# A recurrent attention kernel: three small transfers issued by another engine, and a reordered first step and tail

## The chip, the cores and the metric

The kernel runs on one core of a Trainium2 chip. Its engines each take their instructions in the order written: TensorE (PE: matmuls and transposes; PEld is the loading of its stationary operand), VectorE (DVE), ScalarE (ACT), GpSimd (POOL) and SyncE (SP). DMA transfers are issued by SP, ACT or POOL as instructions in their own streams (SPq, ACTq, POOLq in the views), and carried by 16 DMA engines. The metric is the time of one execution on the device, in microseconds (us).

## The reference

Two blocks read the same normalized rows, and their results are added to the input:

```
x = A_x                                  # 2048 rows of 1024, bf16
xn = layernorm(x)
out = x + A(xn, mem0, Wq, Wk, Wv, Wo) + B(xn, w_r, w_gate, w_up, w_down)
```

A is attention over 64 segments of 32 rows, one after the other, with a memory of 8 rows that each segment rewrites:

```
for s in range(64):
    h = concat(mem, xn[32 rows of segment s])          # 8 + 32 rows
    q, k, v = h @ Wq, h @ Wk, h @ Wv                   # 32 heads of 128
    o = softmax(mask(q k^T / sqrt(128))) v
    o = o @ Wo
    mem = o[:8];  emit o[8:]
```

B picks the two rows with the largest `xn @ w_r`, sends them through a gated feed-forward block of width 3584, scales each by the sigmoid of its score and adds it to that row; all other rows pass through.

## The kernel before

**Segments and left rows.** A step of the loop handles one segment. The segment's outputs that feed the next memory need only 8 memory rows and its first 24 rows, so each step carries 32 rows: 24 of the segment (XM) and 8 of memory. The last 8 rows of every segment (XL), the "left rows", don't depend on the memory for q, k and v. Their q, k and v are computed once, in the first step, for all 64 segments together (512 rows), and stored in DRAM (`ql_d`, `vl_d`). Every later step loads its piece: QKL (128 KB) and VL (64 KB). In each step the left rows also attend; their sums before the output projection (OTL, 64 KB) are stored to `ol_d`, and all 512 rows are projected through Wo in the tail.

**Phases and granules.** The weights are cut into 64 granules of 128 x 2048 (512 KB). A step has six phases of eight granules: phase p is q, k or v for one half of the heads, in the order of `PHASES`: q half 0, k half 0, q half 1, k half 1, v half 0, v half 1. In a phase 32 matmuls (L745) add to PSm. Granules 48 to 63 are Wo, worked through one by one (`w` 0 to 15, L798). 44 granules stay in SBUF; 17 (`streamed`, among them granules 11 and 15) are fetched anew in each step by SP (L388) from copies in DRAM (`wsc`), into five slots; three are kept in part in PSUM and brought back by copies (BK<-KEPT, L411). In the first step the three kept ones are streamed as well (`first_streamed`). `fetch` puts the next streamed granule into a slot; it has to wait until PE is through with what was there.

**Order by hand.** `manual_schedule` leaves each engine's instructions in the order in which the program writes them. Inside a step, `hook(p, kc, fn)` places work behind granule `kc` of phase `p`: the next rows' load at (2, 0), the store of the last step's sums and the load of VL at (2, 2), the transposes of q or k at granule 3 of the phase after theirs, the scores of half 0 at (2, 6) and of half 1 at (4, 6), the attention products at (5, 3), (5, 6) and within Wo at w 5 and w 8. QKL for the next step is loaded at w 9. A phase's result is cast by ACT (XB, L754), transposed by PE (L632), and copied to QT by ACT (L637) or to KT by ACT (its left columns, L640) and DVE (L642).

**The first step.** Its phases are followed by the left rows' products with the same granules: `left_qk` (L500: 16 heads of eight 512-wide matmuls a phase; results cast by ACT at L502 into GA, in the areas `big0` and `big1`), and `left_v`. After phase 1, in the middle of its left products, come the square roots of 15 row tiles' variances (`sd_rows`), `spread` (four small matmuls that lay means and deviations out by segment, and the copies behind them), and 16 router tiles: for each, DVE normalizes 128 rows into XR (L263) and multiplies and sums them with w_r (L265). After phase 1's left products DVE copies the first segment's QKL out of GA (L513). `left_done(p)` does what follows phase p: fetches for the slots that came free, the loading of the areas, the routing of the two rows. `v_homes` lists the resident v granules; its first eight live in the area `big0`, the ninth is granule 43 (`v_homes[8]`), the last one's room (`hx`) holds the router's temporaries first.

**The tail.** After the last step `left_sums` loads the 512 left rows again (XLS, issued by ACT at L850) and normalizes them on DVE (L238 to L864). `left_rows_out(k)`, called for k = 0 and 1, projects two blocks of 128 left rows each: 64 matmuls a block (L874), whose stationary operand is taken out of OTA, where the 128 rows of one head lie 32 elements apart; then two additions on DVE (L880) and a store. Between the two calls, and behind the second, come the gate and up products of the two routed rows (L903), and at the end the down products (L930). Their weights (MW) are loaded by SP into rooms that come free.

Of the kernel before, what the change touches and what calls it, by code (L numbers as in the profile page):

```python
# [20 lines left out]
NEXT_KEPT = 7  # L21
HALF_KEPT = 27
KEPT_HERE = (FIRST_KEPT, NEXT_KEPT, HALF_KEPT)
NEG = -30000.0

PHASES = [(0, 0), (1, 0), (0, 1), (1, 1), (2, 0), (2, 1)]
# [3 lines left out]
def kernel(  # L30
# [94 lines left out]
    def home(g, shape, dtype, name):  # L125
        return wres.tile(shape, dtype, name=name, tag=f"wres{g}")
# [131 lines left out]

    hx = v_homes[-1]

    def router_tile(t):
        XR = home(hx, [P, D], BF16, "XR")
        nc.vector.tensor_scalar(out=XR[:, :], in0=xt(t), scalar1=RI16[:, t, 0:1], scalar2=RI16[:, t, 1:2],  # L263
                                op0=ALU.subtract, op1=ALU.mult)
        nc.vector.tensor_tensor_reduce(out=XR[:, :], in0=XR[:, :], in1=WRB, scale=1.0, scalar=0.0,  # L265
                                       op0=ALU.mult, op1=ALU.add, accum_out=RF[:, t:t + 1])

    def router_out():
        nc.vector.tensor_copy(out=RB, in_=RF)
# [149 lines left out]
        nc.gpsimd.dma_start(out=granule_out(wsc[g], g), in_=granule_dram(g))  # L419

    to_copy = list(streamed)
    flow += [(s, g) for s in range(NSEG) for g in (streamed if s else first_streamed)]

    moe = [("gu", w, kc, fh) for w in range(2) for kc in range(KC) for fh in range(2)]
    moe += [("dn", fg) for fg in range(FC // 2)]
# [50 lines left out]
    first_half(1)  # L476
    nc.sync.dma_start(out=WRB, in_=B_w_r.unsqueeze(0).to_broadcast([P, D]))
    for g in range(KC, 32):
        if g in first_streamed:
            if len(queued) < N_SLOT:  # L480
                fetch()
        else:
            load_resident(g)
        if g >= 8 and g < 15:
            load_x(g - 7)
    for g in v_homes[8:-1]:
        load_resident(g)
    load_parts()

# [3 lines left out]
    def left_qk(mat, half, Gs, between, h0=0, h1=16):  # L493
        if mat == 0 and h0 == 0:
            gathered[half] = area(f"big{half}", [P, NSEG, 256], "GA")
        GA = gathered[half].rearrange("p s (m i q r) -> p s m i q r", m=2, i=4, q=4)
        for h in range(h0, h1):
            PSG = psA.tile([P, 512], F32, tag="acc", name="PSG")
            for kc in range(KC):
                nc.tensor.matmul(PSG[:, :], lhsT=part(Gs[kc], h // 4)[:, P * (h % 4):P * (h % 4 + 1)], rhs=XLT[:, :, kc, :],  # L500
                                 start=(kc == 0), stop=(kc == KC - 1))
            nc.scalar.copy(out=GA[:, :, mat, h % 4, h // 4, :], in_=PSG.rearrange("p (s r) -> p s r", r=XL))  # L502
            if h % 2 == 1 or mat + half == 0:
                next(between, None)
        if h1 < 16:
            return
        for _ in between:
            pass
        if mat == 1:
            G3 = gathered[half]  # L510
            if half == 0:
                qkl[0] = one.tile([P, 2, 2, 4, 4, XL], BF16, tag="bA", name="QKL")
            nc.vector.tensor_copy(out=qkl[0][:, half].rearrange("p m i q r -> p (m i q r)"), in_=G3[:, 0, :])  # L513
            if half == 0:
                for k in range(NSEG // 8):
                    store_left(half, k)
# [30 lines left out]

    def left_done(p):
        for g in range(8 * p, 8 * (p + 1)):
            if g in first_streamed:  # L550
                fetch()
        if p == 1:
            area("big0", [P, 8, 2048], "W8A")
            for g in AREAS["big0"]:
                load_resident(g)
        elif p == 2:
            router_top()
            route_rows()
        elif p == 3:
            route_turns(*routed[0])  # L560
            load_resident(hx)
            home_first()
        elif p == 4:
            area("big1", [P, 8, 2048], "W8B")
        elif p == 5:
            for g in AREAS["pair"][1:] + [hm]:
                load_resident(g)
        if p in (1, 2):
            copy_blocks(6)
# [14 lines left out]

    def load_qkl(s):
        t = qkl[0] = one.tile([P, 2, 2, 4, 4, XL], BF16, tag="bA", name="QKL")
        nc.gpsimd.dma_start(out=t.rearrange("p h m i q r -> p h (m i q r)"),  # L587
                            in_=ql_d[s // 8][:, :, s % 8].rearrange("h p c -> p h c"))

    def load_vl(s):  # L590
        group["vl"] = one.tile([P, 2, P], BF16, tag="vl", name="VL")
        nc.gpsimd.dma_start(out=group["vl"][:, :, :], in_=vl_d[s // 16][:, s % 16, :, :, :])

    def load_left_out(k, queue):
        queue.dma_start(out=areas["big0"][:, 4 * k:4 * k + 4, :], in_=ol_d[k // 4][4 * (k % 4):4 * (k % 4) + 4].rearrange("s p c -> p s c"))
# [5 lines left out]

    def store_sums():
        s, t = unsaved.pop(0)
        nc.gpsimd.dma_start(out=ol_d[s // 16][s % 16], in_=t.rearrange("p r h -> p (r h)"))


    left_stats()
# [13 lines left out]
    for s in range(NSEG):  # L621
# [7 lines left out]
        def transposes(mat, half, XB):  # L629
            PTq = PTB.rearrange("p (i j r) -> p i j r", i=4, j=4)  # L630
            for il in range(4):
                nc.tensor.transpose(out=PTq[:, il, :, :].rearrange("p j r -> p (j r)"), in_=XB[:, il * P:(il + 1) * P],  # L632
                                    identity=IDENT[:, :])
            pv = PTq.rearrange("p i j r -> p (i j) r")
            if mat == 0:
                QT[half] = one.tile([P, 16, 32], BF16, tag="bE", name="QT")
                nc.scalar.copy(out=QT[half][:, :, :], in_=pv)  # L637
            else:
                KT[half] = one.tile([P, 16, NK], BF16, tag="kt", name="KT")
                nc.scalar.copy(out=KT[half].rearrange("p (i q) k -> p i q k", i=4)[:, :, :, 32:NK],  # L640
                               in_=qkl[0][:, half, 1, :, :, :])
                nc.vector.tensor_copy(out=KT[half][:, :, 0:32], in_=pv)  # L642

        def scores(half):
            QKL = qkl[0]
# [92 lines left out]
        for p, (mat, half) in enumerate(PHASES):  # L738
# [13 lines left out]
            if mat < 2:  # L752
                XB = one.tile([P, 512], BF16, tag=("bE", "kt")[mat], name="XB")
                nc.scalar.copy(out=XB[:, :], in_=PSm[:, :])  # L754
                hooks.setdefault((p + 1, 3), []).insert(0, lambda m=mat, h=half, b=XB: transposes(m, h, b))

                if s == 0:
                    Gs = [Gv_ for _, Gv_ in behind]
                    kept = (x for g_, Gv_ in behind if g_ in KEPT_COLS for x in keep(g_, Gv_))
                    h0, h1 = ((8, 16), (0, 1), (0, 4), (0, 8))[p]  # L760
                    left_qk(mat, half, Gs, kept, h0, h1)
                    if p == 1:
                        nc.gpsimd.tensor_copy(out=GATE, in_=gathered[0][:, 0, 128:132])
                        copy_blocks(6)
                        sd_rows(MV[:, 1:NT, :], VE[:, 1:NT])
                        left_qk(mat, half, Gs, kept, 1, 3)
                        h1 = 3
                        spread(1, NT)
                        for t in range(NT):
                            router_tile(t)  # L770
                    elif p == 2:
                        router_out()
                    elif p == 3:
                        routed.append(route())
                    if h1 < 16:
                        left_qk(mat, half, Gs, kept, h1, 16)
            else:
                VM[half] = one.tile([P, 512], BF16, tag="bA", name="VM")
                nc.scalar.copy(out=VM[half][:, :], in_=PSm[:, :])  # L779

                if s == 0:
                    left_v(half, [Gv_ for _, Gv_ in behind])
# [69 lines left out]
    def left_sums():  # L852
# [7 lines left out]
        for t in range(4):  # L860
# [2 lines left out]
            nc.vector.tensor_scalar(out=r, in0=r, scalar1=1.0, scalar2=None, op0=ALU.add)  # L863
            nc.vector.tensor_scalar(out=left_x(t), in0=left_x(t), scalar1=r, scalar2=m, op0=ALU.mult, op1=ALU.add)  # L864

    OTR = OTA.rearrange("p s (r h) -> p (s r) h", h=H)

    def left_rows_out(k):
        WD = [[psK.tile([P, 512], F32, name=f"WD{2 * b + c}", tag=f"kept{2 * b + c}") for c in range(2)] for b in range(2)]
        for b in range(2):  # L870
            for i, (g, Gv) in enumerate(WOS.items()):
                for hs in range(2):
                    for c in range(2):
                        nc.tensor.matmul(WD[b][c][:, :], lhsT=OTR[:, P * (2 * k + b):P * (2 * k + b + 1), 2 * (g - 48) + hs],  # L874
                                         rhs=Gv[:, D * hs + 512 * c:D * hs + 512 * (c + 1)],
                                         start=(i + hs == 0), stop=(i == 15 and hs == 1))
            x = left_x(2 * k + b)
            for c in range(2):
                xc = x[:, 512 * c:512 * (c + 1)]
                nc.vector.tensor_tensor(out=xc, in0=xc, in1=WD[b][c][:, :], op=ALU.add)  # L880
            nc.scalar.dma_start(out=out2.rearrange("(t s r) d -> t s r d", t=4, s=16)[2 * k + b, :, XM:SEG, :], in_=x)

    T0 = room(resident[2], "T0")
    left_sums()
    left_rows_out(0)
    ROW = T0[:, 0:256]
# [85 lines left out]
```

## Time and profile before

| | us |
|---|---|
| median of 3 runs | 1849.24 (1846.27 to 1857.47) |
| the profiled execution | 1847.92 |
| its span, first to last instruction | 1846.3 |
| first step ends (first L828) | 241.0 |
| last of the 64 steps ends (last L828) | 1759.9 |
| PE busy, of the span | 1555.7 (84%) |
| DVE, ACT, POOL busy | 880.4, 774.9, 320.9 |
| mean granted clock of TensorE | 0.982 |

The rows of the profile are read like this. A line number is a line of the kernel, `out<-in` names its tiles, `xN` counts instructions. In a view in order of time the first column is the start in us from the span's start, the second the duration; a bracket at the end says how long the engine stood idle before it and for whom. In the waits the columns are the sum in us, the count and the longest. In a row of one line the three numbers are the shortest, median and longest duration in ns, then the first and last start. In a row of DMA issues the last two columns are the size of each and the median us from issue to landing.

### The profile page before, as it was taken

The numbers are of one execution on the slowest core, as the hardware profiler recorded it, in microseconds if no ns is written. First come the engines' busy times: TensorE is split into PE (matmuls) and PEld (weight loads), VectorE is DVE, ScalarE is ACT, GpSimd is POOL, SyncE is SP. The second block draws the span as 40 slices with busy tenths as digits, with TensorE's granted clock in tenths as the row PEclk, the third lists the DMA queues.
The fourth block names the chain that finished last, engine by engine and source line by source line (L and its number), as shares of the span: only waits on it lengthen the run. The fifth ranks groups of instructions, "written<-read, shape, count | busy, mean of one in ns | idle before, by whom it ended". The sixth has DMA issues, their size and how long they took to land. (4 is left out here: it accounts for less than half of the span.)

```text
span 1846.3 us, 70379 instructions
## 1 busy us (share of the span) xinstructions
PE 1555.7 (84%) x30358; PEld 828.2 (45%) x30370; DVE 880.4 (48%) x2711; ACT 774.9 (42%) x2019; POOL 320.9 (17%) x592
## 2 busy tenths in 40 slices
PE   6889978888888888888888888888888888888888
PEld 3334434444444444444444444444444444444465
DVE  6631235555554454555555555444455555555420
ACT  2333134444444444444444444444444444444400
POOL 1020111111111111111111111111111111111200
PEclk9999989999999999999999999999999999999988
DMA  9684899999999999999999999999999999999996
GB/s 361 218 301 135 261 367 391 393 394 394 368 387 376 368 389 383 392 386 372 396 393 396 396 394 394 385 386 389 386 391 394 397 382 393 395 395 395 392 364 251
DMA packets 223288, 678.50 MB, mean 367 GB/s; under 512 B 46848, under 2 KB 54320, under 8 KB 222976
## 3 DMA queue, kind: packets, MB, share of 16 engines
q1 hardware_dynamic: 196768, 623.79, 88.3%
q0 software_dynamic: 24192, 46.54, 7.5%
q8 instruction: 237, 3.88, 0.8%
q10 hardware_dynamic: 2016, 3.67, 0.6%
q14 instruction: 75, 0.61, 0.1%
HBM read 652.90 MB, written 29.89 MB: 370 GB/s over the span
## 5 line engine op out<-in xcount | busy, mean ns | idle before, releaser
L745 PE MATMUL PSm<-wres,ST 128*32 128x512 bf16 x6400 | 500.7, 382 | 0.0
L745 PEld LDWEIGHTS <-ST 128*32 128x32 bf16 x12288 | 313.3, 96 | 349.5 <-issue 107.4
L745 PE MATMUL PSm<-g,ST 128*32 128x512 bf16 x3084 | 307.3, 384 | 46.6 <-DMA g<-wsc 38.2
L411 ACT COPY BK<-KEPT 128x512 bf16<-128x512 bf16 x315 | 189.3, 601 | 175.0 <-PE WO L798 65.1
L798 PEld LDWEIGHTS <-OT 128*32 128x32 bf16 x8192 | 209.2, 97 | 85.6 <-issue 69.3
L754 ACT CAST XB<-PSm 128x512 bf16<-128x512 f32 x256 | 150.2, 587 | 132.7 <-PE PSm L745 131.1
L642 DVE COPY KT<-BT 128x512 bf16<-128x512 bf16 x128 | 51.8, 405 | 290.6 <-PE BT L632 290.6
L798 PE MATMUL WO<-W8B,OT 128*32 128x256 bf16 x4096 | 186.2, 276 | 0.0
L745 PE MATMUL PSm<-W8A,ST 128*32 128x512 bf16 x2048 | 182.7, 380 | 0.0
L587 POOL DMA_DIRECT2D QKL<-ql_d x63 | 46.5, 738 | 755.7 <-ACT OTL L714 740.6
L798 PE MATMUL WO<-g,OT 128*32 128x256 bf16 x2560 | 130.7, 277 | 53.1 <-DMA g<-wsc 48.8
L832 POOL DMA_DIRECT2D out_dram<-XN x256 | 130.7, 526 | 173.9 <-DVE XN L828 173.8
L779 ACT CAST VM<-PSm 128x512 bf16<-128x512 f32 x128 | 80.3, 627 | 114.0 <-PE PSm L745 114.0
L411 DVE COPY BK<-KEPT 128x512 bf16<-128x512 bf16 x189 | 80.2, 425 | 72.3 <-ACT BK L411 36.9
L632 PEld LDWEIGHTS <-XB 128*128 128x128 bf16 x1024 | 57.9, 98 | 106.6 <-ACT XB L754 101.5
L674 DVE TENSOR_REDUCE DN<-BS 128x8 f32<-128x320 f32 x128 | 62.9, 491 | 88.0 <-ACT BS L669 88.0
L632 PE MATMUL BT<-IDENT,XB 128*128 128x128 bf16 x1024 | 101.7, 222 | 3.1
L500 PE MATMUL PSG<-XLT,wres 128*128 128x512 bf16 x352 | 101.3, 390 | 0.8 <-ACT GA L502 0.7
L637 ACT COPY QT<-BT 128x512 bf16<-128x512 bf16 x128 | 74.9, 585 | 53.4 <-PE BT L632 51.4
L659 DVE TENSOR_TENSOR BS<-BS,CT 128x96 f32<-128x96 f32 (+1 forms) x256 | 59.7, 233 | 76.5 <-PE BS L652 72.0
L745 PE MATMUL PSm<-BK,ST 128*32 128x512 bf16 x567 | 76.7, 388 | 22.2 <-DVE ST L369 22.2
L828 DVE CAST XN<-WO 128x256 bf16<-128x256 f32 x64 | 27.2, 424 | 127.5 <-PE WO L798 127.5
(171 smaller groups left out, 2278.9 us busy)
## 6 DMA issues: line engine op xcount, KB each, us to landing
g<-wsc SPq DMA_DIRECT2D x1071, 512.0 KB, 6.3
ql_d<-GA POOLq DMA_DIRECT2D x16, 512.0 KB, 6.3
QKL<-ql_d POOLq DMA_DIRECT2D x63, 128.0 KB, 6.2
MW<-in_B_w_gate_dram SPq DMA_DIRECT2D x16, 448.0 KB, 8.0
MW<-in_B_w_down_dram SPq DMA_DIRECT2D x14, 512.0 KB, 8.3
wres<-in_A_Wk_dram SPq DMA_DIRECT2D x12, 512.0 KB, 10.5
MW<-in_B_w_up_dram SPq DMA_DIRECT2D x12, 448.0 KB, 8.5
XP<-in_A_x_dram SPq DMA_DIRECT2D x8, 512.0 KB, 10.1
```

The lines of the kernel that those rows point to most:

```text
L411: copy(out=back[g][c], in_=KEPT_COLS[g][c])
L500: nc.tensor.matmul(PSG[:, :], lhsT=part(Gs[kc], h // 4)[:, P * (h % 4):P * (h % 4 + 1)], rhs=XLT[:, :, kc, :], start=(kc == 0), stop=(kc = ...
L632: nc.tensor.transpose(out=PTq[:, il, :, :].rearrange("p j r -> p (j r)"), in_=XB[:, il * P:(il + 1) * P], identity=IDENT[:, :])
L637: nc.scalar.copy(out=QT[half][:, :, :], in_=pv)
L642: nc.vector.tensor_copy(out=KT[half][:, :, 0:32], in_=pv)
L659: nc.vector.tensor_tensor(out=S4, in0=S4, in1=m, op=ALU.add)
L674: nc.vector.tensor_reduce(out=DN[:, :], in_=S8, axis=AX.X, op=ALU.add)
L745: nc.tensor.matmul(PSm[32 * jq:32 * jq + 32, :], lhsT=ST[:, kc, :], rhs=part(Gv, jq), start=(kc == 0), stop=(kc == KC - 1), tile_position= ...
L754: nc.scalar.copy(out=XB[:, :], in_=PSm[:, :])
L779: nc.scalar.copy(out=VM[half][:, :], in_=PSm[:, :])
L798: nc.tensor.matmul(PS[32 * g:32 * g + 32, 0:256], lhsT=lhs(h), rhs=Gv[:, D * hs + 256 * g:D * hs + 256 * (g + 1)], start=False, stop=(last ...
L832: nc.gpsimd.dma_start(out=out2[s * SEG:s * SEG + XM, 256 * g:256 * (g + 1)], in_=OB[32 * g:32 * g + XM, :])
```

## The change

- In the first step granule 15 (GUEST) is not streamed but loaded with the resident ones, into the room of granule 43; granule 43 is loaded into that room after phase 1.
- `sd_rows` and `spread` for tiles 1 to 15 and the router's tiles move from the middle of phase 1's left products to the end of phase 0's; the tiles alternate between two halves of XR.
- In the first step QKL's copy and the main part of KT's copy are done by ACT, not DVE.
- In all steps QKL's load, VL's load and the store of the left sums are issued by ACT, not POOL.
- In the tail DVE first copies the two heads of a Wo granule for 128 left rows into OCS (eight pieces in turn, in the room that T0 had), and the matmuls of L874 read their stationary operand there, contiguous. T0 moves to another tile.

```diff
-    def router_tile(t):
-        XR = home(hx, [P, D], BF16, "XR")
+    def router_tiles():
+        XR = home(hx, [P, 2, D], BF16, "XR")
+        for t in range(NT):
...
-    flow += [(s, g) for s in range(NSEG) for g in (streamed if s else first_streamed)]
+    flow += [(s, g) for s in range(NSEG) for g in (streamed if s else first_streamed) if s or g != GUEST]
...
     for g in range(KC, 32):
-        if g in first_streamed:
+        if g == GUEST:
+            t = res_tiles[g] = room(v_homes[8], "guest")
+            nc.sync.dma_start(out=t, in_=granule_dram(g))
+        elif g in first_streamed:
             if len(queued) < N_SLOT:
                 fetch()
...
-    for g in v_homes[8:-1]:
+    for g in v_homes[9:-1]:
         load_resident(g)
...
-            nc.vector.tensor_copy(out=qkl[0][:, half].rearrange("p m i q r -> p (m i q r)"), in_=G3[:, 0, :])
+            nc.scalar.copy(out=qkl[0][:, half].rearrange("p m i q r -> p (m i q r)"), in_=G3[:, 0, :])
...
     def left_done(p):
         for g in range(8 * p, 8 * (p + 1)):
-            if g in first_streamed:
+            if g in first_streamed and g != GUEST:
                 fetch()
-        if p == 1:
+        if p == 0:
+            sd_rows(MV[:, 1:NT, :], VE[:, 1:NT])
+            spread(1, NT)
+            router_tiles()
+        elif p == 1:
+            res_tiles.pop(GUEST)
+            load_resident(v_homes[8])
             area("big0", [P, 8, 2048], "W8A")
...
     def load_qkl(s):
-        nc.gpsimd.dma_start(out=t.rearrange("p h m i q r -> p h (m i q r)"),
+        nc.scalar.dma_start(out=t.rearrange("p h m i q r -> p h (m i q r)"),
...
     def load_vl(s):
-        nc.gpsimd.dma_start(out=group["vl"][:, :, :], in_=vl_d[s // 16][:, s % 16, :, :, :])
+        nc.scalar.dma_start(out=group["vl"][:, :, :], in_=vl_d[s // 16][:, s % 16, :, :, :])
...
     def store_sums():
-        nc.gpsimd.dma_start(out=ol_d[s // 16][s % 16], in_=t.rearrange("p r h -> p (r h)"))
+        nc.scalar.dma_start(out=ol_d[s // 16][s % 16], in_=t.rearrange("p r h -> p (r h)"))
...
-                nc.vector.tensor_copy(out=KT[half][:, :, 0:32], in_=pv)
+                (nc.vector.tensor_copy if s else nc.scalar.copy)(out=KT[half][:, :, 0:32], in_=pv)
...
-                        sd_rows(MV[:, 1:NT, :], VE[:, 1:NT])
-                        left_qk(mat, half, Gs, kept, 1, 3)
-                        h1 = 3
-                        spread(1, NT)
-                        for t in range(NT):
-                            router_tile(t)
...
+    OCS = room(resident[2], "OCS").rearrange("p (n h r) -> p n h r", n=8, h=2)
...
         for b in range(2):
             for i, (g, Gv) in enumerate(WOS.items()):
+                OC = OCS[:, (16 * (2 * k + b) + i) % 8]
+                h = 2 * (g - 48)
+                nc.vector.tensor_copy(out=OC, in_=OTR[:, P * (2 * k + b):P * (2 * k + b + 1), h:h + 2].rearrange("p r h -> p h r"))
                 for hs in range(2):
                     for c in range(2):
-                        nc.tensor.matmul(WD[b][c][:, :], lhsT=OTR[:, P * (2 * k + b):P * (2 * k + b + 1), 2 * (g - 48) + hs],
+                        nc.tensor.matmul(WD[b][c][:, :], lhsT=OC[:, hs, :],
...
-    T0 = room(resident[2], "T0")
+    T0 = one.tile([P, 256], BF16, tag="bA", name="T0")
     left_sums()
     left_rows_out(0)
```

More of the change, by code (lines that the diff above doesn't have):

```diff
@@ L23 @@
 KEPT_HERE = (FIRST_KEPT, NEXT_KEPT, HALF_KEPT)
+GUEST = 15
 NEG = -30000.0
@@ L259 @@
     hx = v_homes[-1]
-    def router_tile(t):
-        XR = home(hx, [P, D], BF16, "XR")
[L263 to L266, printed above, removed]
+    def router_tiles():
+        XR = home(hx, [P, 2, D], BF16, "XR")
+        for t in range(NT):
+            nc.vector.tensor_scalar(
+                out=XR[:, t % 2, :], in0=xt(t), scalar1=RI16[:, t, 0:1], scalar2=RI16[:, t, 1:2],
+                op0=ALU.subtract, op1=ALU.mult)
+            nc.vector.tensor_tensor_reduce(out=XR[:, t % 2, :], in0=XR[:, t % 2, :], in1=WRB, scale=1.0, scalar=0.0,
+                                           op0=ALU.mult, op1=ALU.add, accum_out=RF[:, t:t + 1])
     def router_out():
```

## The prediction

> **What bounds the kernel now.** I read the page, then the stretches (columns: length; busy time of PE, weight loads, VectorE (DVE), ScalarE (ACT) and GpSimd (POOL) with instruction counts; granted clock, DMA share, GB/s), then the waits, then first step and tail in order of time. The profiled execution took 1847.92 us (span 1846.3), 1.3 under the median of 1849.24.
>
> ```profile
> GB/s 361 218 301 135 261 367 391 393 394 394 368 387 376 368 389 383 392 386 372 396 393 396 396 394 394 385 386 389 386 391 394 397 382 393 395 395 395 392 364 251
> ```
> ```profile
> 265.00:1750.00 1485.00, 1249.47 (x27650) 666.57 (x27649) 753.53 (x2407) 690.50 (x1854) 276.39 (x499) 1.00 1.02 389
> ```
> ```profile
> L828 DVE CAST XN<-WO x64: 423/424/425, 241.0 to 1759.9; 128x256 bf16<-128x256 f32 x64
> ```
>
> L828 ends each step: the first at 241.0, then 63 more take (1759.9 - 241.0)/63 = 24.11 us each, and the tail lasts 86 us. In the 63 steps the DMA engines are full (share 1.02, 389 GB/s) while PE is busy for 1249 of 1485 us. There a wait taken from PE buys nothing by itself; fewer bytes, or bytes that move faster, do.
>
> ```profile
> 53.06 0.83 PE L745 MATMUL PSm<-wres,ST 128*32 128x512 bf16 x12
> ...
> 60.73 0.62 PE L745 MATMUL PSm<-g,ST 128*32 128x512 bf16 x4 [5.54 <-DMA g<-in_A_Wk_dram]
> ...
> 99.93 0.23 PE L650 MATMUL BS<-KT,QT 128*32 128x40 bf16 x4 [6.73 <-ACT KT L640]
> ```
> ```profile
> 60.00:64.00 4.00, 3.27 (x11) 1.14 (x11) 0.00 (x0) 0.58 (x1) 0.00 (x0) 0.50 0.65 260
> ```
>
> In the first step PE is the path, with two holes: from 55.2 it lacks granule 15 for 5.54 us, from 93.2 it lacks KT for 6.73 us. Behind a hole the granted clock is 0.50 (60 to 64), so each hole also costs about 2 us of work done at half speed.
>
> ```profile
> 1760.19 9.28 PE L874 MATMUL WD<-W8B,OTA 128*128 128x512 bf16 x31 [0.37 <-issue]
> ...
> 1776.22 7.07 PE L874 MATMUL WD<-W8B,OTA 128*128 128x512 bf16 x32
> ...
> 1790.03 6.20 PE L903 MATMUL GU<-RXT,MW 128*128 128x2 bf16 x233
> 1797.54 1.39 PE L903 MATMUL GU<-RXT,MW 128*128 128x2 bf16 x47 [1.31 <-issue]
> ```
> ```profile
> 1770.73 1.29 DVE L238 BATCH_NORM_STATS2 T<-XLS 128x6 f32<-128x512 bf16 x2 [0.43 <-DMA XLS<-in_A_x_dram]
> ...
> 1777.43 0.55 DVE L864 TENSOR_SCALAR XLS<-XLS,T 128x1024 bf16<-128x1024 bf16 x1
> 1777.89 1.28 DVE L880 TENSOR_TENSOR XLS<-XLS,WD 128x512 bf16<-128x512 bf16 x2
> ```
>
> In the tail PE is the path too: left-row products (L874) from 1760.19, gate and up from 1790, then the other half. Meanwhile DVE normalizes the left rows: the last of them arrive by DMA at 1770.7, the last L864 ends at 1777.98. Until L880, PE needs none of that.
>
> **First step: the guest.** Granule 15 is loaded within the initial stream into the room of granule 43, and not into a stream slot that comes free at the end of phase 0. The 5.54 us go, and some 2 us of half clock behind them. Granule 43 is loaded after phase 1 and first used in phase 5, behind three phases of 27.6 us of products (below), so at nothing; were it late after all, PE would wait for one landing, once.
>
> **First step: the router.** Today it stands on DVE ahead of QKL's copy and KT's:
>
> ```profile
> 53.44 0.18 DVE L242 TENSOR_SCALAR MISC<-MISC 128x15 bf16<-128x15 bf16 x1
> 68.78 0.87 DVE L255 COPY BS<-BT 96x30 f32<-96x30 f32 x4 [15.16 <-PE BT L250]
> ...
> 99.27 0.22 DVE L513 COPY QKL<-GA 128x256 bf16<-128x256 bf16 x1
> 99.40 0.42 DVE L642 COPY KT<-BT 128x512 bf16<-128x512 bf16 x1
> ```
> ```profile
> 998.62 0.58 ACT L754 CAST XB<-PSm 128x512 bf16<-128x512 f32 x1 [0.35 <-PE PSm L745]
> 999.84 0.30 ACT L640 COPY KT<-QKL 128x128 bf16<-128x128 bf16 x1 [0.64 <-PE BT L632]
> ```
>
> Spread copies and sixteen tiles take 99.27 - 68.78 = 30.5 us. Moved behind phase 0, the square root can start when L242 ends (53.62) and spread's products near 54.1. PE is free at 53.0 and waits 1.1 us: a new wait, with all of phase 1 behind it on PE. DVE is then done at 54.4 + 30.5 = 85. A head product costs PE 0.216 us (in the tail 64 of the same width take from 1776.22 to 1790.03), so phase 1 with its 2.4 us (2.1 to the hole, 0.3 for the last granule) and 16 x 8 products, 27.6, ends near 84.4, and PE asks for KT near 86. Both copies are now on ACT, 0.3 and 0.6 by the two rows above, behind the last head's cast: PE waits some 0.6 us in place of 6.73, without the clock loss, and DVE is just free for the mask. Sum: -(5.5 + 2) - (6.7 + 1.8) + 1.1 + 0.6 = **-14 us** (what follows in this step is released by PE and moves along; -9 if a load there comes late, -16 at best).
>
> **Loop: three transfers from ACT.**
>
> ```profile
> QKL<-ql_d POOLq DMA_DIRECT2D x63, 128.0 KB, 6.2
> ...
> ol_d<-OTL POOLq DMA_DIRECT2D x64, 64.0 KB, 5.3
> VL<-vl_d POOLq DMA_DIRECT2D x63, 64.0 KB, 5.9
> ```
> ```profile
> L850 ACTq DMA_DIRECT2D XLS<-in_A_x_dram x4: 574/612/1272, 1752.3 to 1754.9; - x4
> ```
> ```profile
> PE WO L798 <- DMA g<-wsc: 43.4, 83, 1.8
> PE PSm L745 <- DMA g<-wsc: 35.8, 83, 1.5
> ...
> PE WO L703 <- DMA VL<-vl_d: 15.5, 17, 2.8
> ```
> ```profile
> PEld L703 <- DMA VL<-vl_d: 33.3, 37, 3.3
> ```
>
> An issue on ACT costs about 0.6 us (L850). The store of sums and VL come between XB's dispatch at 998.62 and KT's copy at 999.84: 1.2 us of issue in 1.2 us of room, so KT slips by 0 to 0.6 us, and behind it stand a KEPT copy, XB and QT. QKL's issue waits for PE's attend, whose results ACT has just copied; behind it stand a KEPT copy and ST, neither urgent. The cover: between 300 and 1700 us (58 steps) PE waits 79.2 us for streamed weights, 1.4 a step, and 48.8 for VL, 0.8 a step. VL no longer stands behind the next rows' load on POOL, so most of the 0.8 goes; what comes late next is the streamed weight. Without that cover 0.6 x 63 = 38 us would show.
>
> What counts is how fast the engines move these runs of 512 bytes when POOL isn't the issuer. The nearest rows are eight OTA loads from SP (4096 such runs) after 1788, and eight from POOL with the left rows beside them before 1768:
>
> ```profile
> 1780.00:1788.00 8.00, 7.95 (x38) 5.32 (x38) 0.00 (x0) 0.00 (x0) 0.00 (x0) 1.00 1.03 408
> 1788.00:1800.00 12.00, 10.54 (x293) 9.17 (x293) 1.28 (x2) 0.00 (x0) 0.00 (x0) 0.68 1.12 346
> 1750.00:1768.00 18.00, 13.67 (x172) 8.14 (x163) 4.53 (x12) 1.20 (x5) 5.33 (x9) 0.72 1.04 334
> ```
>
> From SP the rate falls from 408 to 346 for 12 us: 1.8 us lost, 0.44 ns a run; the 512 runs of a step would lose 0.22 us, 14 us over the loop. From POOL it is 334, no better, so the price of the move may be 0. It may be below 0: the slices of the page fall to 368 in places where a late VL may leave slots idle, and 1485 us at 393 and not 389 are 15 us less. I take **+6 us**, between POOL's price and SP's; ends -15 and +14. The Trainium skill (DMA: Bandwidth & Descriptors, Rules for kernel authors) says that spreading DMAs over SP, ACT and GpSimd saves only issue time, since all run on the same 16 engines; by it this term would be 0 and the sum 6 lower.
>
> **Tail.**
>
> ```profile
> L874 PEld LDWEIGHTS <-OTA x256: 136/144/170, 1759.8 to 1827.9; 128*128 128x128 bf16 x128
> ```
>
> The strided weight loads cost nothing now: 144 ns lie under 216 ns of product, so making them contiguous gains 0. The 64 copies themselves (256 elements, about 0.3 us each, between the 0.22 and 0.42 of the two copies on DVE above) lie beside 0.86 us of products each. Their order costs: the first is emitted behind the left rows' normalization, on the same engine. L874 can't start at 1760.2; DVE is free at 1778, and the left rows come about 1 us later, since ACT first issues the store of the last sums. First copy near 1779.3, first product near 1779.7: **+19.5 us**, all on the path, for gate and up stand behind L874 on PE. The 1.3 us at 1797.5 come back, those weights having long landed. And the copies for a half's second row block stand behind L880 of its first (1.28 us), so PE stands about 2 us, twice, with a chance of half clock behind it (0.72 was granted in 1750 to 1768, among such holes), put at 0.85 each: +5.7. The Trainium skill (TensorE: Matmul & The Clock Gate, Part 1) lets the clock fall only after an idle window of 3.4 us; by it the 1.7 us of clock would be 0. Sum: 19.5 - 1.3 + 5.7 = **+24**, from +18 (left rows sooner, full clock) to +27.
>
> **Sum.** -14 + 6 + 24 = +16 on 1847.9 is 1864; with the 1.3 to the median, **1865 us**.
>
> **Rivals.**
> 1. Slower loop: a run from ACT costs what SP's did. -14 + 14 + 24 = +24, 1873. For it, the 346 GB/s; against, POOL's 334. Chance 0.22.
> 2. The stall is hidden: the routed rows' weights, not PE, hold the end, and the tail adds only the row-block holes less 1.3, +4. -14 + 6 + 4 = -4, 1845, no slower than before. It decides where these weights would land over 20 us behind PE's need; against it, PE waits 1.3 us for them. Chance 0.10.
> 3. Faster loop: with these rows out of POOL's queue all steps run at the best slice, 397: 1485 x (1 - 389/397) = 30. -14 - 30 + 24 = -20, 1829. Against: the share is 1.02 already. The Trainium skill (DMA: Bandwidth & Descriptors, Latency and other measured facts) guesses that GpSimd's descriptor rings slow two of the engines; no row here shows engines singly. Chance 0.08.
> 4. ACT becomes the bound: its three issues, 1.8 us a step by L850's median, outgrow the cover of 2.2. At 0.9 us an issue (its longest is 1.27) 0.5 us a step show: +32 more, 1897. Chance 0.05.
>
> The forecast itself has 0.55, from 1852 to 1873. About 1% is what a measurement can tell from no change: 1831 to 1867.7 here. Of the forecast's 0.55, 0.35 lies under 1867.7. Same: 0.35 + 0.10 (rival 2) + 0.03 (rival 1's lower edge) = 0.48; slower 0.20 + 0.19 + 0.05 = 0.44; faster 0.08. The range 1842 to 1881 takes in the forecast and rivals 1 and 2, and leaves out 3, 4 and edges.
>
> **What would show it.** No hole on PE at 55, short ones at 53 and 86, the first L828 near 227. Steps of 24.2 us at a DMA share of 1.02, and no VL among PE's waits. The first L874 some 19 us behind the last L828, and holes of 2 us between row blocks. I am wrong if L874 starts at once, if a step changes by over 0.3 us, or if the first step ends above 235.

## The result and the profile after

The changed kernel took 1880.17 us (median of 4 runs, 1868.25 to 1891.65), the kernel before 1850.97 beside it. The ratio is 1.0147, with an interval of 1.0100 to 1.0195: slower by about 1.5%. The profiled execution took 1878.1 us (span 1876.5).

The diff shifts the lines: L828 is now L834, L745 L757, L798 L804, L874 L884, L388 L391; the new copies of the tail are L881. First the row of the line that ends each step (columns as in the prediction):

```profile
L834 DVE CAST XN<-WO x64: 424/425/426, 224.9 to 1766.5; 128x256 bf16<-128x256 f32 x64
```

It splits the 30.2 us between the two spans:

| | before | after | difference | forecast |
|---|---|---|---|---|
| first step, to the first L834 | 241.0 | 224.9 | -16.1 | -14 |
| 63 steps, and one step | 1518.9, 24.11 | 1541.6, 24.47 | +22.7 | +6 |
| tail, from the last L834 | 86.4 | 110.0 | +23.6 | +24 |

**First step.** In order of time, these are PE's rows where the two holes of 5.54 and 6.73 us had been (the bracket is the idle time ahead and its releaser):

```profile
52.35 0.25 PE L251 MATMUL BT<-MISC 128*128 128x30 bf16 x4 [0.80 <-ACT MISC L244]
...
84.96 0.21 PE L662 MATMUL BS<-KT,QT 128*32 128x40 bf16 x4 [0.17 <-ACT KT L654]
```

Granule 15 is there in time, so no row near 55 us has a bracket. The scores wait 0.17 us for KT.

**Loop.** The page's slices of the DMA rate, the stretch from 265 to 1750 us, and PE's waits between 300 and 1700 us:

```profile
GB/s 359 286 269 192 300 374 383 383 387 383 382 376 377 372 380 367 374 394 393 381 377 383 382 373 372 391 392 395 386 380 392 392 390 394 390 377 383 349 292 161
```
```profile
265.00:1750.00 1485.00, 1247.41 (x27304) 661.58 (x27286) 743.05 (x2375) 691.65 (x1829) 153.46 (x304) 1.00 1.01 383
```
```profile
PE WO L804 <- DMA g<-wsc: 59.1, 110, 2.2
PE PSm L757 <- DMA g<-wsc: 51.3, 112, 1.5
...
PE BS L662 <- ACT KT L652: 1.1, 4, 0.4
```

PE waits 110.4 us for streamed weights where it had waited 79.2. VL no longer stands among its waits. The engines move 383 GB/s in place of 389, 1.5% less, and the step is 1.5% longer. These waits tell where the loss arises, not its size: by the rows from 265 to 1750, at 24.11 and 24.47 us a step, PE is idle for 3.82 us a step before and 3.92 after, and busy for 20.29 and 20.55. The ends of products are modelled in the profile, so a short stall may stand in either. What is new stands in another engine's list, that of SP's own waits in the same stretch (sum, count, longest):

```profile
SPq L391 <- PE PSm L757: 334.1, 526, 1.9
...
SPq L391 <- DMA QKL<-ql_d: 103.4, 58, 3.8
SPq L391 <- DMA ol_d<-OTL: 103.0, 57, 3.3
...
SPq L391 <- DMA VL<-vl_d: 12.7, 18, 2.3
```

SP issues only the weight fetches here (L391). These need neither QKL nor OTL nor VL, and yet SP stands 219.1 us waiting until those transfers have landed; the kernel before has no such row. Not all of that is lost, since SP had to wait for PE to free a slot anyway. In the kernel before that wait was

```profile
SPq L388 <- PE PSm L745: 453.4, 640, 3.9
```

and it is now 119 us shorter. The trace's records of the transfers' issue show why SP waits. They are abridged here: waits of 17 ns, the other instructions of ACT, and whatever stands at "..." are left out. Columns: start in us, duration in ns, what the instruction is (for a wait, the semaphores that it waits for), and the semaphore that the transfer will count up when it lands:

```
SP   1003.00   320  fetch                      semaphore=100
SP   1004.87   320  fetch                      semaphore=102
SP   1006.03   319  fetch                      semaphore=104
SP   1007.30   320  fetch                      semaphore=105
ACT  1007.85   377  QKL load                   semaphore=103
SP   1008.12   320  fetch                      semaphore=106
SP   1009.13   320  fetch                      semaphore=107
SP   1010.55   320  fetch                      semaphore=108
SP   1012.34   320  fetch                      semaphore=100
SP   1013.43  2389  wait  $S[105]>= $S[103]>=
SP   1015.85   320  fetch                      semaphore=103
...
ACT  1017.31   344  OTL store                  semaphore=102
...
SP   1022.06  1595  wait  $S[105]>= $S[102]>=
SP   1023.69   320  fetch                      semaphore=102
```

In this trace all transfers issued by SP and by ACT count up one of the same eight semaphores (100 and 102 to 108), which they take in turn. A fetch whose turn falls on 103 waits until the last user of 103 has landed. That was the QKL load, issued at 1007.85, after the fetches that hold the next two turns (104 and 105). The last count for it came at 1015.80, 8.0 us later, and SP's wait ends at 1015.82. The median is 7.2 us:

```profile
QKL<-ql_d ACTq DMA_DIRECT2D x63, 128.0 KB, 7.2
...
ol_d<-OTL ACTq DMA_DIRECT2D x64, 64.0 KB, 6.6
VL<-vl_d ACTq DMA_DIRECT2D x63, 64.0 KB, 7.6
```

GpSimd's transfers use none of these eight (theirs are 109 to 116). Every fetch stands in order behind the waiting one. The Trainium skill (DMA: Bandwidth & Descriptors, Anatomy of one DMA, which follows GpSimd's path) says that DMA engines don't wait on semaphores and that the sequencer which issues waits ahead of the dispatch; the trace agrees, since it is SP that stands, for 2.39 us here.

**Tail.** PE and DVE in order of time:

```profile
1765.86 0.62 PE L804 MATMUL WO<-g,OT 128*32 128x256 bf16 x8 [1.76 <-DMA g<-wsc]
1787.48 8.92 PE L884 MATMUL WD<-W8B,OCS 128*128 128x512 bf16 x32 [21.00 <-DVE OCS L881]
...
1804.76 7.08 PE L884 MATMUL WD<-W8B,OCS 128*128 128x512 bf16 x32 [1.45 <-DVE OCS L881]
...
1827.63 1.34 PE L913 MATMUL GU<-RXT,MW 128*128 128x2 bf16 x45 [2.86 <-issue]
...
1845.90 7.08 PE L884 MATMUL WD<-W8B,OCS 128*128 128x512 bf16 x32 [1.45 <-DVE OCS L881]
```
```profile
1766.53 0.42 DVE L834 CAST XN<-WO 128x256 bf16<-128x256 f32 x1 [6.79 <-PE WO L804]
1773.28 1.29 DVE L239 BATCH_NORM_STATS2 T<-XLS 128x6 f32<-128x512 bf16 x2 [6.32 <-DMA XLS<-in_A_x_dram]
...
1786.59 0.55 DVE L870 TENSOR_SCALAR XLS<-XLS,T 128x1024 bf16<-128x1024 bf16 x1
1787.05 2.73 DVE L881 COPY OCS<-OTA 128x256 bf16<-128x256 bf16 x9
```

PE stands for 21.00 us. DVE first waits 6.32 us for the left rows, normalizes them until 1787, and only then begins the copies on which the first product depends. Twice more PE stands 1.45 us between two row blocks.

### The profile page after: what moved, and what is told of

Same layout as the page of the kernel before. It is cut to its first block, busy times and chain, and to the rows that moved or that the text cites. A ratio compares the mean times of both kernels' runs of the same rounds, so it can differ in the third digit from the quotient of the medians.

```text
span 1876.5 us, 70496 instructions
## 1 busy us (share of the span) xinstructions
PE 1565.5 (83%) x30370; PEld 817.6 (44%) x30370; DVE 899.8 (48%) x2771; ACT 787.7 (42%) x2023; POOL 200.5 (11%) x402
## 4 chain that ended last, share of the span: by engine, by line
DMA 47%; PE 39%; DVE 7%; ACT 5%; issue 2%; ACTq 0%; SPq 0%; DVEq 0%
DMA g<-wsc 43%; PE PSm L757 16%; PE PSG L506 6%; PE WO L804 5%; PE WD L884 3%; PE PSV L533 2%; PE BT L644 2%; ACT BS L681 1%; DMA XLS<-in_A_x_dram 1%; DMA ol_d<-OTL 1%; DMA QKL<-ql_d 1%; PE BT L348 1%; ACT OTL L726 1%; PE BS L662 1%; ACT OT L724 1%
## 5 line engine op out<-in xcount | busy, mean ns | idle before, releaser
L757 PE MATMUL PSm<-wres,ST 128*32 128x512 bf16 x6400 | 501.9, 384 | 0.0
L757 PEld LDWEIGHTS <-ST 128*32 128x32 bf16 x12288 | 313.3, 96 | 379.8 <-issue 141.8
L757 PE MATMUL PSm<-g,ST 128*32 128x512 bf16 x3080 | 307.9, 386 | 61.9 <-DMA g<-wsc 55.3
L414 ACT COPY BK<-KEPT 128x512 bf16<-128x512 bf16 x315 | 185.0, 587 | 176.5 <-PE WO L804 66.5
L804 PEld LDWEIGHTS <-OT 128*32 128x32 bf16 x8192 | 208.4, 97 | 109.8 <-issue 95.3
L804 PE MATMUL WO<-g,OT 128*32 128x256 bf16 x2560 | 130.0, 276 | 74.6 <-DMA g<-wsc 68.6
L804 PE MATMUL WO<-W8B,OT 128*32 128x256 bf16 x4096 | 184.4, 274 | 0.0
L757 PE MATMUL PSm<-W8A,ST 128*32 128x512 bf16 x2048 | 182.9, 381 | 0.0
L757 PE MATMUL PSm<-BK,ST 128*32 128x512 bf16 x567 | 76.6, 391 | 22.5 <-DVE ST L372 22.5
L834 DVE CAST XN<-WO 128x256 bf16<-128x256 f32 x64 | 27.2, 425 | 134.5 <-PE WO L804 134.5
L724 ACT CAST OT<-BS 128x128 bf16<-128x128 f32 x130 | 34.6, 266 | 116.0 <-PE BT L718 114.8
```

The source lines that it names most:

```text
L414: copy(out=back[g][c], in_=KEPT_COLS[g][c])
L757: nc.tensor.matmul(PSm[32 * jq:32 * jq + 32, :], lhsT=ST[:, kc, :], rhs=part(Gv, jq), start=(kc == 0), stop=(kc == KC - 1), tile_position= ...
L804: nc.tensor.matmul(PS[32 * g:32 * g + 32, 0:256], lhsT=lhs(h), rhs=Gv[:, D * hs + 256 * g:D * hs + 256 * (g + 1)], start=False, stop=(last ...
```

## The experiments

**Theories.** For the loop: A, the shared semaphores hold up SP's fetches; B, runs of 512 bytes cost more DMA time when ACT issues them; C, something else in the change. For the tail: the order on DVE, or the copies themselves. For the first step: guest, early router and copies on ACT, each with the forecast's price. Each kernel that was timed more than once has a ratio to the kernel before, run beside it.

### The queue undone: queue_back

```diff
-        nc.scalar.dma_start(out=t.rearrange("p h m i q r -> p h (m i q r)"),
+        nc.gpsimd.dma_start(out=t.rearrange("p h m i q r -> p h (m i q r)"),
```

and the same for VL's load and OTL's store.

> The three small transfers of a step (QKL and VL loads, OTL store) go back to GpSimd's queue; first step and tail stay as in the changed kernel (profiled 1878.1 us, 24.47 us a step from the first to the last normalisation, kernel before 24.11). Theory A, shared completion semaphores (SyncE's granule fetch has to wait until the small ScalarE transfer that used the same semaphore has landed: 103.4 + 103.0 + 12.7 us of such waits on SyncE's queue between 300 and 1700 us): the rows of SyncE waiting for QKL, OTL and VL are gone, the step is 24.1 (24.05 to 24.2), the time 1878 - 22 = 1856 (1851 to 1862). Theory B, 512-byte runs (the small transfers take more DMA time when ScalarE issues them): the same time, so this run does not tell A from B. Theory C, the loop is slower for another reason of the change (the first step leaves other buffers, ScalarE's program is another): the step stays above 24.35 and the time above 1870.

```profile
L834 DVE CAST XN<-WO x64: 424/425/426, 228.3 to 1752.5; 128x256 bf16<-128x256 f32 x64
```

24.19 us a step, no wait of SP for a small transfer, ratio 1.0018 (0.9981 to 1.0054). The 1862.51 us lie 0.5 above A's window, but the kernel before took 1858.38 here and not 1850.97, so ratios are compared from here on. The changed kernel's 1.0147 less this is 1.3%, or 24 us; with the two intervals apart it is at least 0.0046 x 1850 = 8.5. So the queue is what the loop lost by; C falls.

### Half of it: qkl_on_pool and vl_otl_on_pool

The same edit for QKL alone, and for VL and OTL alone.

> Only the QKL load goes back to GpSimd; VL and OTL stay on ScalarE. Theory A: the OTL store now has one more granule fetch (1.3 us) between it and the next transfer on its semaphore, so its wait on SyncE falls from 1.8 us a time to about 0.5, and the QKL wait is gone: step 24.1 to 24.25, time about 1861 (1854 to 1866), that is, over three quarters of the 22 us come back with half of the bytes. Theory B: by bytes, QKL is 128 of 256 KB, half of it comes back: step 24.3, time 1867.

> VL and OTL go back to GpSimd; QKL stays on ScalarE. Theory A: one more granule fetch lies between QKL and the next transfer on its semaphore, the wait falls from 1.8 us to between 0.5 and 1, step 24.1 to 24.3, time about 1862 (1855 to 1868); together with the kernel that puts QKL alone back, the two savings add up to well over the 22 us (30 or more), since each removes most of the other's wait too. Theory B: half of the bytes, step 24.3, time 1867, and the two savings add up to the 22 us.

SP's waits with QKL on GpSimd, then with VL and OTL there:

```profile
SPq L391 <- DMA ol_d<-OTL: 81.6, 58, 3.5
...
SPq L391 <- DMA VL<-vl_d: 5.3, 7, 1.0
```
```profile
SPq L391 <- DMA QKL<-ql_d: 39.6, 38, 2.6
```

The ratios are 1.0018 (0.9986 to 1.0049) and 1.0002 (0.9971 to 1.0033): either half, taken away alone, brings back all that the whole does, 24 and 27 us, as A said of their sum. By bytes each should have left half of the loss, a ratio near 1.008, outside both intervals. That speaks against B, but at the smallest price that the intervals allow, half of it would be a ratio of 1.004, inside the first; the next pair decides. The step of qkl_on_pool missed A's window: its traced 24.30 us is what B said. That trace was taken in an execution of 1873.38 us, against a median of 1860.20, and the ten runs count for more. The step of vl_otl_on_pool, 24.01, lies below A's 24.1. OTL's wait also fell less than A said (to 1.4 us a time, not 0.5), and still the 1.5 us a step of waits that SP has left cost no time that shows. SP has slack to cover them: its waits for PE's products are 399.0 us in this kernel, 451.8 in queue_back.

### Two more turns a step: two_tiny, and its control two_tiny_pool

```diff
+        for i in range(2):
+            nc.sync.dma_start(out=tiny_d[i:i + 1, :], in_=r_d[:, 64 * i:64 * i + 64])
```

behind QKL's load in `load_qkl` (`tiny_d` is a new DRAM tile that nothing reads); in the control QKL, VL and OTL are on GpSimd as well.

> The changed kernel with two more transfers of 128 bytes each (DRAM to DRAM) issued by SyncE behind the QKL load in the program of every step; nothing reads what they write. Theory A: they use up two of the eight semaphores, so two fetches (2.7 us) fewer lie between QKL, or OTL, and the next transfer on its semaphore: SyncE's waits for QKL grow from 1.8 us a time to above 3.5, the step grows by 0.5 us or more (25.0 and above), the time is 1910 us or more. Theory B: the bytes are nothing (256 of 9 MB a step) and the issues cost SyncE 0.3 us each beside its slack: step at most 24.6, time at most 1886.

> The control to the kernel with two tiny transfers a step (25.58 us a step, 1955.6 us): the same two transfers of 128 bytes on SyncE, but QKL, VL and OTL are back on GpSimd. Theory A (what costs is that SyncE's fetches wait on semaphores that the small ScalarE transfers hold): no rows of SyncE waiting for QKL, OTL or VL, step 24.1 to 24.4 as without the tiny transfers (24.19), time at most 1872. Rival (the tiny transfers themselves cost: two issues and two landings a step in SyncE's order): step above 25.0, time above 1915.

With the tiny transfers, SP's waits and the step line; then the step line of the control:

```profile
SPq L392 <- DMA QKL<-ql_d: 198.4, 55, 5.3
...
SPq L392 <- DMA ol_d<-OTL: 85.5, 44, 3.4
SPq L392 <- DMA VL<-vl_d: 51.0, 43, 2.1
```
```profile
L837 DVE CAST XN<-WO x64: 424/425/426, 227.6 to 1839.4; 128x256 bf16<-128x256 f32 x64
```
```profile
L837 DVE CAST XN<-WO x64: 423/425/426, 228.3 to 1781.1; 128x256 bf16<-128x256 f32 x64
```

256 bytes a step cost 75 us over the changed kernel's median: 1955.58, ratio 1.0528 (1.0470 to 1.0586), 25.58 us a step. SP waits 3.6 us for each QKL. The control, a single run, has no wait for QKL, OTL or VL, but it missed A's windows for step and time: 24.65 us a step and 1889.76 us. It did not reach the rival's 25.0 and 1915 either. So the two tiny transfers cost by themselves, by this run some 0.45 us a step over 24.19; why is open. The two kernels that differ only in who issues the three small transfers took 1951.6 and 1889.8 us in their profiled runs, a difference of 62 us. They ran on two chips, on which the kernel before took 1858.38 and 1856.32. Without the tiny transfers the same difference was 18 by the medians and 24 by the ratios. So the price of the move to ACT grows to 2.6 to 3.5 times when two more transfers a step take their turns, and a price by bytes would have stayed as it was. Theory A stands.

| kernel | SP's waits for small transfers, us a step (300 to 1700) | step, us |
|---|---|---|
| queue_back | 0 | 24.19 |
| vl_otl_on_pool | 39.6 / 58.3 = 0.7 | 24.01 |
| qkl_on_pool | 86.9 / 57.6 = 1.5 | 24.30 |
| sums_spread (below; its loop is the changed kernel's) | 215.0 / 57.5 = 3.7 | 24.34 |
| changed kernel | 219.1 / 57.2 = 3.8 | 24.47 |
| two_tiny | 334.9 / 54.7 = 6.1 | 25.58, of it 0.45 the tiny transfers' own |

Each step is read off one trace. Kernels that leave all three transfers with GpSimd have 24.11 (the kernel before) to 24.39 us (copies_only, below), so of these rows only two_tiny's stands clear, and the 0.36 us between the two main traces is not far above that spread. The price rests on the ratios. A second pair of them agrees: sums_spread has its transfers on ACT and a tail of 96.5 us, 12.7 shorter than queue_back's 109.2, and yet its ratio is 0.0034 higher, which is 6 us. Its loop thus costs some 19 us more (10 to 28 by the two intervals together).

### The tail's order alone: sums_spread

```diff
-    left_sums()
+    sums_parts = left_sums_parts()
     left_rows_out(0)
...
+                if k == 0 and i >= 6:
+                    next(sums_parts, None)
```

`left_sums_parts` is `left_sums` cut into nine pieces, of which each `next` emits one.

> The changed kernel, its contiguous copies kept; only the order on VectorE is another: the normalisation of the left rows is emitted in nine pieces between the copies 7 to 15 of the first row block, and not ahead of the first copy. Theory order (the tail's +23.6 us is the first copy waiting on VectorE for 19.5 us behind the normalisation, with holes between row blocks of 1.45 us): the first left-row product starts within 2 us of the last normalisation (before 0.3, changed 21), the holes of 1.45 us between row blocks stay, the tail is 89 to 95 us in place of 110.0, the time 1878 - 18 = 1860. Theory copies (the copies themselves, or the products that read them, are what is slow): the tail stays above 103.

PE in order of time:

```profile
1760.83 8.72 PE L887 MATMUL WD<-W8B,OCS 128*128 128x512 bf16 x31 [1.21 <-DVE OCS L884]
...
1770.73 1.04 PE L887 MATMUL WD<-XLT,OCS 128*128 128x512 bf16 x4 [1.18 <-DVE OCS L884]
...
1773.12 1.04 PE L887 MATMUL WD<-XLT,OCS 128*128 128x512 bf16 x4 [1.35 <-DVE OCS L884]
...
1774.79 1.88 PE L887 MATMUL WD<-wres,OCS 128*128 128x512 bf16 x4 [0.64 <-DVE OCS L884]
...
1784.04 6.22 PE L887 MATMUL WD<-W8B,OCS 128*128 128x512 bf16 x28 [1.45 <-DVE OCS L884]
```

The 21 us are gone: the first product waits 1.21 us. The tail is 1856.2 - 1759.7 = 96.5, so 13.5 of the 23.6 come back. The ratio is 1.0052 (1.0019 to 1.0084), 1861 us. The tail missed its 89 to 95: the pieces of the normalization wait for the left rows' transfers, copies stand behind them, and PE waits 1.18, 1.35 and 0.64 us for these. Order is the main cause: it explains 13.5 of the 23.6. With the copies kept the tail is still 10 us longer than before, and 7 of these stand in the first two row blocks (1760.8 to 1797.9, against 1760.2 to 1790.0), where these waits are. This kernel issues QKL, VL and OTL from ACT, and SP waits 215 us for them as in the changed kernel (rows not shown).

### The first step alone: first_step_only and first_again

Queue as in queue_back, and in the tail:

```diff
-                OC = OCS[:, (16 * (2 * k + b) + i) % 8]
...
-                        nc.tensor.matmul(WD[b][c][:, :], lhsT=OC[:, hs, :],
+                        nc.tensor.matmul(WD[b][c][:, :], lhsT=OTR[:, P * (2 * k + b):P * (2 * k + b + 1), 2 * (g - 48) + hs],
```

> Both the queue and the tail are undone: the three small transfers are on GpSimd's queue, the left-row products read OTA with the stride of the kernel before; guest, early router and the copies on ScalarE stay. If the three parts add up as the traces say: first normalisation at 225 to 229 us (before 241.0), step 24.1, tail 86 to 87 us, so 12 to 16 us less than before: ratio about 0.992 (0.988 to 0.997). Rival, what the first step gains is given back in the loop (the stream begins sooner but is bound by the DMA engines all the same): step 24.3 or more, ratio 0.998 to 1.003.

> The kernel with the first step's changes alone once more, beside the kernel before on the same chip, for a closer interval (0.9888, 0.9812 to 0.9964 so far): 13 us less by its trace, ratio 0.990 to 0.996.

The ratios are 0.9888 (0.9812 to 0.9964) and, in six runs, 0.9899 (0.9863 to 0.9934): 1836.5 against 1856.32 us. This version beats both kernels. Its step line in the second run, span 1841.2:

```profile
L834 DVE CAST XN<-WO x64: 423/425/426, 228.6 to 1755.7; 128x256 bf16<-128x256 f32 x64
```

First step -12.4, tail 85.5, steps 24.24. Since the strided weight loads are back and the tail is as short as before, the contiguous copies buy nothing. The rival had the first step's gain given back in the loop. The traced steps, 24.28 and 24.24, are nearer to its 24.3 than to the expected 24.1, but the time is not: the ratios are below the rival's 0.998, and 0.9899, a hair under the expected 0.990, means 19 us less, 6 more than the first step explains. Where these 6 come from is open.

### The first step's parts: router_back, no_guest, copies_only

On top of first_step_only: the router in phase 1 again; granule 15 by a stream slot again (`GUEST = -1`); both.

> As the kernel with the first step's changes alone, but with the router's square root, spread and sixteen tiles on VectorE back in the second phase, as before; the guest stays and the KT and QKL copies of the first step stay on ScalarE. By the forecast's term for the router (6.7 us of hole, 1.8 of clock, less 1.1 and 0.6 of new waits) the hole of 6 to 7 us comes back where VectorE is done with the tiles (99 us), now at the mask or at the KT copy, and the first normalisation moves from 225 to 229 us to some 7 later, 232 to 236. Rival (the copies on ScalarE alone take the hole away): it stays at 226 to 230.

> As the kernel with the first step's changes alone, but granule 15 is fetched into a stream slot behind phase 0 as before; the early router and the copies on ScalarE stay. By the forecast's term for the guest (5.5 us of hole, 2 of clock): TensorE waits again some 5.5 us for the granule at 55 us, and the first normalisation moves by 5 to 8 us, to 231 to 236. Rival (the early router's own waits cover that hole, or the first step is bound by its loads further on): under 3 us.

> Of the whole change only the QKL and KT copies of the first step on ScalarE are left (and the router's second scratch row): granule 15 by a stream slot, router in the second phase, queue and tail as before. By the two runs before (guest 5.9 us: 233.7 against 227.8; early router 1.7 us: 229.5 against 227.8) the first normalisation comes at 227.8 + 5.9 + 1.7 = 235.4 (233 to 237.5), some 5.6 us sooner than in the kernel before (241.0); the hole of 4 to 6 us at 55 us is there, the hole of 6.7 us ahead of the first scores is not. If the parts need each other (with the guest's hole back the router runs later, to 97 us or so, and the mask behind it holds something up): 238 or later.

Their step lines, in that order:

```profile
L837 DVE CAST XN<-WO x64: 423/425/426, 229.5 to 1758.6; 128x256 bf16<-128x256 f32 x64
```
```profile
L834 DVE CAST XN<-WO x64: 423/425/426, 233.7 to 1763.5; 128x256 bf16<-128x256 f32 x64
```
```profile
L837 DVE CAST XN<-WO x64: 423/425/426, 235.3 to 1771.7; 128x256 bf16<-128x256 f32 x64
```

Against 227.8, the guest is worth 5.9 us; the hole is back in its place, at 4.56 us. The early router is worth 1.7. With both undone it ends at 235.3, so the two copies on ACT are worth 241.0 - 235.3 = 5.7. Each of these is the difference of two single traces, and kernels with the same first step end it between 224.9 and 229.0; the router's 1.7 is lost in that spread, the other two are rough. The expectations for no_guest and copies_only held; that for router_back failed and its rival held. The DVE and PE rows of router_back show why:

```profile
88.67 0.54 DVE L265 TENSOR_SCALAR XR<-XP,MISC 128x1024 bf16<-128x1024 bf16 x1
...
90.39 0.26 DVE L669 TENSOR_TENSOR BS<-BS,CT 128x96 f32<-128x96 f32 x1
```
```profile
86.40 0.21 PE L660 MATMUL BS<-KT,QT 128*32 128x40 bf16 x4 [0.17 <-ACT KT L652]
```

The mask (L669) does wait on DVE behind the router until 90.39. But PE needs only KT for the scores at 86.40, which ACT copies, and then has phase 2's left products to do. No run has the early router with the copies left on DVE, so whether that alone would also fill the hole of 6.73 us isn't known.

### QKL alone from ACT: qkl_on_act

first_step_only with QKL's load on ACT.

> The first step's changes and only the QKL load on ScalarE (VL and OTL on GpSimd, tail as before). Theory A: SyncE still waits for QKL in some steps (39.6 us in all in the kernel that had this queue with the changed tail, at 24.01 us a step), DMA engines stay full; step 24.0 to 24.3, no difference to the kernel with the first step's changes alone that 5 rounds can tell: ratio 0.986 to 0.996. Theory B (512-byte runs from ScalarE cost by bytes): 11 us more than without, ratio above 0.996.

The ratio is 0.9908 (0.9874 to 0.9943), no different from first_again on the same chip: a load on ACT for which SP waits only 48.2 us (300 to 1700) costs nothing that shows, and gains nothing. B's 11 us aren't there. The profiled execution was the slowest of its six (1853.27 us) by one hole in the tail, 9.00 us for OTA rows from GpSimd's queue. That hole was seen once and its cause is open.

## Why the prediction was right or wrong

The forecast was 1865 us, from 1842 to 1881. The 1880.17 us lie inside the range, at its edge, 15 above the forecast. "Slower" had 0.44, a little less than "same". Two of the three terms came out near their size, in part by luck, and the third missed its own range.

- **First step, -14.** Measured -16.1 in this trace and -12 to -16 in others with the same first step. The size was right, one of its two reasons doubtful. The guest's 5.5 + 2 measured 5.9. The router's 6.7 + 1.8 less 1.1 and 0.6 is had for the most part by the copies on ACT alone, 5.7; with them in place the router's move adds 1.7 at most. The forecast treated the router and the copies as one, because KT's copy stood behind the router on DVE. Moving the copy off that queue is enough; that moving the router would have been enough too is not shown.
- **Loop, +6 between -15 and +14.** Here the forecast failed. By the two traces it is +22.7; the queue's price is 24 by the ratio of queue_back, and at least 8.5. The step at fault is "What counts is how fast the engines move these runs of 512 bytes when POOL isn't the issuer": it priced bytes and ACT's own time, and did not ask what SP's stream waits for. In its place comes SP waiting 3.8 us a step for transfers that it doesn't need. Rival 1 (1873) was nearest in time, but by the price of runs, which the half-moves and two_tiny with its control refuted. VL's wait on PE did go, as said, and bought nothing, the stream being late in its place. Rival 4 fell: by their medians ACT's three issues took 0.38, 0.34 and 0.56 us, 1.28 a step and not 1.8, and PE waited 1.1 us in all for ACT's part of KT. By the Trainium skill (DMA: Bandwidth & Descriptors, Rules for kernel authors), as quoted for this term, it would have been 0. That fits the bytes, which cost nothing that shows in qkl_on_act, and not the loop, which lost some 23 us by the semaphores.
- **Tail, +24.** Measured +23.6. That it is so near is partly luck, since its parts were off both ways. "First product some 19 us behind" became 21.0, since the left rows came later. The holes between row blocks are 1.45 us each, not 2, and behind them 32 products take 7.08 us, 0.22 each, at a granted clock of 1.00 (1804.7 to 1811.7): no half clock. So the forecast's 5.7 is 2.9. By the Trainium skill (TensorE: Matmul & The Clock Gate, Part 1), with its idle window of 3.4 us, the clock part was 0; behind these holes the trace agrees. Elsewhere in this tail the clock fell without idle time: it is 0.50 from 1822.4 to 1824.7, where PE is busy all through with products of two columns. "The 1.3 us at 1797.5 come back" was wrong: the hole ahead of the last gate and up products is 2.86 us now, though the last of their weights were issued by 1790.2 and none took over 13.3 us. What the page calls "issue" there stays open.
- **Its own tests.** First L834 below 235, no start of L884 at once: right. "If a step changes by over 0.3 us": it changed by 0.36, and the loop was what was wrong, though single traces of loops that should be alike differ by nearly as much (24.11 to 24.39).

## What to carry to other kernels

A transfer that is moved to another queue can also change which completion semaphore it holds, as here, and so who waits for whom. Where a stream of fetches bounds the kernel, read the waits of its own queue in the profile, and keep slow, late transfers off the semaphores that the stream takes in turn. Where an engine's queue holds up an operand, try to move the operand's copy before the work ahead of it; and before copies go in to make an operand contiguous, look whether its loads are hidden already, and what stands ahead of the first copy on its engine.

## What the runs showed that was not expected

Two transfers of 128 bytes a step, on an engine with slack, made the step some 0.45 us longer, in one run, even where nothing waited for them by name; with the small ScalarE transfers in the same rotation it was 1.1 us (25.58 against 24.47). And the small transfers took longer from issue to landing from ScalarE than from GpSimd in the loop: QKL 7.2 us against 6.2, VL 7.6 against 5.9, OTL 6.6 against 5.3.
